# Keeping background work out of the step ahead of an accumulator copy, and computing the last output chunk in two halves

## The chip, the cores and the metric

The kernel is one program on one core of a Trainium2 chip. The metric is the device time of one execution in microseconds; of several executions the median is taken. The engines are named as in the profile: PE (matrix multiplications; PEld is its weight loads), DVE (the vector engine), ACT (the scalar engine), POOL (here the issuer of the stores to DRAM) and SP (the issuer of the loads and of the output stores). Each engine works through its own instructions strictly in order; an instruction that waits for a semaphore holds back all that stand behind it on that engine.

## What is computed

```python
# attention, B,H,S,Ns,D = 4,8,512,32,64, both ways, with softmax
xread = softmax(x @ state.T / 8) @ state      # x rows
sread = softmax(state @ x.T / 8) @ x          # state rows
x = concat(xread, sread)  ->  (2304, 512)
# first MLP, 512 -> 2048 -> 512
h = x @ w_in;  x = (h - tanh(h)) @ w_out
# second MLP, 512 -> 2048 -> 512
h = x @ w_in2; out = (h * tanh(softplus(h))) @ w_out2
```

The weights of the program arrive as 64-bit floats and are read as pairs of 32-bit words. The result is 32-bit.

## The kernel before, in words

Products are made to near 32-bit precision out of three products of a large part and a small remainder (`mm3p`, line 647): large x large, large x small, small x large. So nearly every tensor is split first: ACT copies the large part (names ending in `h`: `gh`, `wh`, `swh`, `yh`), and DVE subtracts it to get the rest (`gl`, `wl`, `swl`, `yl`).

The first MLP is a loop of 68 steps (lines 1217 to 1226), over `seq`: 16 tiles of 128 hidden columns for each of the batches 0, 1 and 2, then 4 tiles "s" for the state rows of all batches, then 16 tiles for batch 3. Batch 2 begins with step 32, "s" with step 48, batch 3 with step 52. A step does, in program order: `up` of its tile (6 matmuls into one of the two banks `h0`, `h1`; ACT takes the tanh, DVE subtracts it from the bank, which frees the bank, then ACT and DVE split it into `gh`, `gl`); the side work due at that step (the attention of the next batch; the products `swp`, whose two results lie in two side banks and are split into `swh`, `swl`; transposes `xtp`, which use the same two side banks in turn); `down` of a tile three steps back (`LA` is 3; near the end up to five), 12 matmuls into the four accumulator banks `a0` to `a3`; and `keep_pace` (line 1101), which runs some pieces of background work.

After the 16th `down` of a batch its four banks are copied out, two by ACT and two by DVE (line 713), and the first `down` of the next batch has to wait for these copies. That happens at steps 34 (batch 1), 50 (batch 2) and 54 (the state rows: one bank, `a3`, copied by ACT to `ys`, line 748).

A piece of background work converts or splits a part of the second MLP's weights and stores it to DRAM by POOL, from which it is loaded again later; or it prepares the second MLP's input of batches 0 and 1 (`pieces_y`). A conversion is two ACT operations on a loaded tile (`w<-st`, `r<-st`), one DVE operation and the load of a later tile; a split is one ACT and one DVE operation and two stores. There are 94 pieces. `keep_pace` runs them up to a goal that rises by 2.2 per step, at most `MOST` = 3 in a step (4 from step 58), and only while ten SBUF slots are free. Where a piece's new tile gets the slot of a tile that was stored, its first operation waits for the landing of that store.

After the first steps the order on an engine is not the program's: a scheduler places each instruction when its own count of time has its inputs ready. A piece can so stand on ACT or DVE ahead of an earlier step's operation.

The second MLP follows as 16 groups (`group`, line 940), PE-bound, with `down_2` (line 894) for the output chunks of 128 rows: 6 matmuls of 512 columns into one of three banks, then DVE adds the bank to the sum so far. In the last group the sum is stored. The very last chunk was computed like the others; only its addition and store were made in two halves of 256 columns (lines 921 to 925).

Of the kernel before, what the change touches and what calls it, by code (L numbers as in the profile page):

```python
# [17 lines left out]
LA = 3  # L18
# [8 lines left out]
MOST = 3  # L27
# [47 lines left out]
def attention_moe_kernel(  # L75
# [41 lines left out]
    def get(name, dtype=F32, newest=False):  # L117
        if halves and dtype == F32:
            return halves.popleft()
        i = free.pop() if newest else free.popleft()  # L120
        return Unit(slots.tile([128, 512], dtype, tag=f"k{i}", name=name), i)

    def put(*units):
        for u in units:
            if u.slot is None:
                halves.append(u)
            else:
                free.append(u.slot)
# [44 lines left out]
    last = [None]  # L173
# [74 lines left out]
    def run_piece():  # L248


        bg.popleft()()
        now[0] += 1
        send(now[0] - 1, now[0] - HOLD)

    def send(ready, gone):
        while stores and stores[0][0] < ready:
            _, u, d = stores.popleft()
            v = u.t.bitcast(F32)
            nc.gpsimd.dma_start(  # L259
                out=d, in_=v if len(d.shape) == 2 else v.rearrange("p (g e) -> p g e", g=2)  # L260
            )
            sent.append((now[0], u))
        while sent and sent[0][0] < gone:
            put(sent.popleft()[1])
# [382 lines left out]
    def mm3p(o, lh, ll, rh, rl, start, stop, **kw):  # L647
        TE.matmul(out=o, lhsT=lh, rhs=rh, start=start, stop=False, **kw)
        TE.matmul(out=o, lhsT=lh, rhs=rl, start=False, stop=False, **kw)
        TE.matmul(out=o, lhsT=ll, rhs=rh, start=False, stop=stop, **kw)  # L650
# [36 lines left out]
    def evac(dst, src, i):  # L687
        if i % 2:
            return V.tensor_copy(out=dst, in_=src)
        return AC.activation(out=dst, in_=src, func=ACTF.Copy)  # L690
# [139 lines left out]
    W2, O2, G2, OUT = {}, {}, {}, {}  # L830
# [63 lines left out]
    def down_2(g, b, r, gs, last):  # L894
        d_n[0] += 1
        ps = psum.tile([128, 512], F32, tag=DB[d_n[0] % len(DB)], name="acc")
        for f in range(2):
            if b == "s":
                gh, gl = (x.t[:, f * 128:(f + 1) * 128] for x in gs["s"])
            else:  # L900
                gh, gl = (x.t[:, r * 128:(r + 1) * 128] for x in gs[f, b % 2])
            wh, wl = O2[2 * g + f]
            mm3p(ps, gh, gl, wh.t, wl.t, f == 0, f == 1)
        if g == 0:
            OUT[b, r] = get("out")
            evac(OUT[b, r].t, ps, r)
            return
        o = OUT[b, r]
        if g < NT // 2 - 1:
            V.tensor_tensor(out=o.t, in0=ps, in1=o.t, op=ALU.add)  # L910
            return
        OUT.pop((b, r))
        if b == "s":
            V.tensor_tensor(out=o.t, in0=ps, in1=o.t, op=ALU.add)
            for bb in range(B):
                nc.sync.dma_start(
                    out=out[bb * T + S:(bb + 1) * T, :], in_=o.t[bb * NS:(bb + 1) * NS, :]
                )
        else:
            rows_out = out[b * T:b * T + S, :].rearrange("(p r) d -> p r d", r=4)[:, r, :]  # L920
            n = 2 if last else 1
            for j in range(n):
                c = slice(j * 512 // n, (j + 1) * 512 // n)
                V.tensor_tensor(out=o.t[:, c], in0=ps[:, c], in1=o.t[:, c], op=ALU.add)
                nc.sync.dma_start(out=rows_out[:, c], in_=o.t[:, c])
        put(o)
# [70 lines left out]
    def downs(u, g, with_s, last=False):  # L997
        gs = {k: G2.pop(k) for k in list(G2)}
        order = [(2 * u + 1, r) for r in range(4)]
        order += [("s", 0)] if with_s else []  # L1000
        order += [(2 * u, r) for r in range(4)]
        done = []

        def one(i):
            down_2(g, *order[i], gs, last and i == len(order) - 1)
            done.append(i)
            if len(done) == len(order):
                for x in gs.values():
                    put(*x)
                put(*O2.pop(2 * g), *O2.pop(2 * g + 1))  # L1010

        return [lambda i=i: one(i) for i in range(len(order))]
# [52 lines left out]
    start = {}  # L1065
# [35 lines left out]
    def keep_pace(i):  # L1101
        for (s0, n0), (s1, n1) in zip(pace, pace[1:]):
            if s0 <= i < s1:
                goal = n0 + (n1 - n0) * (i + 1 - s0) / (s1 - s0)
                ran = done[0]
                for _ in range(MOST + (i >= start[3] + 6)):
                    if done[0] < goal and bg and len(free) >= RESERVE:
                        run_piece()
                        done[0] += 1
                if ran == done[0]:  # L1110
                    now[0] += 3
                    send(now[0], now[0] - HOLD)
# [105 lines left out]
    for i, q in enumerate(seq):  # L1218
        marks.append([e.recent for e in engines])
        up(q)  # L1220
        for f in side.pop(i, []):
            f()
        while low <= i - LA - max(0, BACK - (len(seq) - 1 - i) // 2):
            down(seq[low])
            low += 1
        keep_pace(i)
# [65 lines left out]
```

## Time and profile before

| | us |
|---|---|
| median of 3 runs | 724.94 |
| lowest, highest | 724.18, 726.45 |
| the profiled execution itself | 724.73 |
| its span, first to last instruction | 723.0 |
| PE busy in the span | 709.4 |
| DVE busy, ACT busy | 465.6, 353.5 |

The granted clock of PE is 0.998 of full speed over the span, the upper of its two levels. The three runs lie 2.3 us apart. Nearly all instructions are recorded by one helper and carry its line, L62, so tiles tell them apart. Steps 30 to 68 of the first MLP lie from about 180 to 350 us, the second MLP behind them.

### The profile page before, as it was taken

The page shows a single profiled execution, that of the slowest core. Times are in us where ns is not written, and L with a number is a line of the kernel's source. Part 1 is how long each engine was busy: PE and PEld are TensorE (multiplying, and loading weights), DVE is VectorE, ACT ScalarE, POOL GpSimd, SP SyncE. Part 2 cuts the span into 40 slices and gives each one's busy share as a digit, 9 for nine tenths or more (in the row PEclk, how much of TensorE's full clock was granted, in tenths as well). Part 3 has the DMA queues.
Part 4 walks back from the last instruction along what each step waited for, and adds up shares of the span by engine and source line. Part 5 has one row for each costly group of instructions (what it writes and reads, how often), then busy time and mean ns, then how long its engine had stood idle before and what let it go on. Part 6 is the DMA issues. An engine that isn't in the chain of part 4 may idle for free.

```text
span 723.0 us, 10559 instructions
## 1 busy us (share of the span) xinstructions
PE 709.4 (98%) x3968; PEld 567.2 (78%) x3968; DVE 465.6 (64%) x793; ACT 353.5 (49%) x631; POOL 70.5 (10%) x110
## 2 busy tenths in 40 slices
PE   8899999999999999999999999999999999999997
PEld 6467877778777898777878888888788888888886
DVE  5899755575667748798557775556753365445654
ACT  6998455555675647676637332324433323222320
POOL 0000010012412214412004000000000000000000
PEclk9999999999999999999999999999999999999999
DMA  9984120023753439664958644454766354422003
GB/s 292 332 299 169 59 59 1 31 63 114 262 186 135 160 99 309 231 222 140 393 224 278 217 155 146 139 173 146 267 227 213 94 162 137 140 88 73 1 1 131
DMA packets 52643, 118.66 MB, mean 164 GB/s; under 512 B 7280, under 2 KB 11632, under 8 KB 52592
## 3 DMA queue, kind: packets, MB, share of 16 engines
q1 hardware_dynamic: 44272, 90.72, 38.4%
q0 software_dynamic: 8320, 27.27, 10.4%
q8 instruction: 31, 0.51, 0.3%
q14 instruction: 20, 0.16, 0.1%
HBM read 88.34 MB, written 29.62 MB: 163 GB/s over the span
## 4 chain that ended last, share of the span: by engine, by line
PE 68%; issue 13%; DVE 7%; ACT 6%; POOL 4%; DMA 0%; POOLq 0%; DVEq 0%; ACTq 0%
PE acc L62 35%; PE h L62 26%; POOL wi L259 3%; ACT w L62 2%; PE hs L62 2%; ACT r L62 1%; DVE wide L62 1%; DVE gl L62 1%; POOL wo L259 1%; PE xtp L62 1%; PE swp L62 1%; DVE yl L62 1%; PE srd L62 1%; DVE t L62 1%; DVE wl L62 1%
## 5 line engine op out<-in xcount | busy, mean ns | idle before, releaser
L62 PE MATMUL acc<-wo,gh 128*128 128x512 f32 x544 | 167.9, 390 | 0.0
L62 PE MATMUL h<-yh,ws 128*128 128x512 f32 x448 | 157.0, 392 | 0.5 <-DVE wide L62 0.5
L62 PEld LDWEIGHTS acc<-wo,gh 128*128 128x128 f32 x544 | 101.5, 188 | 21.1 <-ACT gh L62 0.5
L62 PE MATMUL acc<-wo,gl 128*128 128x512 f32 x272 | 106.0, 390 | 0.5 <-DVE gl L62 0.5
L62 DVE TENSOR_TENSOR wide<-acc,wide 128x512 f32<-128x512 f32 (+1 forms) x92 | 62.7, 684 | 62.5 <-PE acc L62 60.9
L62 PE MATMUL acc<-gh,wh 128*128 128x512 f32 x244 | 99.2, 407 | 0.7 <-ACT wide L62 0.4
L62 PEld LDWEIGHTS h<-yh,ws 128*128 128x128 f32 x448 | 84.1, 188 | 18.9 <-DVE wide L62 1.7
L62 PE MATMUL acc<-gh,wl 128*128 128x512 f32 x244 | 95.5, 391 | 0.0
L62 PE MATMUL acc<-gl,wh 128*128 128x512 f32 x244 | 95.4, 391 | 0.0
L62 DVE TENSOR_TENSOR wide<-h,wide 128x512 f32<-128x512 f32 x98 | 67.4, 688 | 31.8 <-ACT wide L62 18.8
L62 PE MATMUL h<-yl,ws 128*128 128x512 f32 x224 | 87.3, 390 | 0.0
L62 DVE TENSOR_TENSOR gl<-wide,gh 128x512 fp32r<-128x512 f32 x76 | 52.5, 690 | 37.7 <-ACT gh L62 36.8
L62 ACT ACTIVATE wide<-wide 128x512 f32<-128x512 f32 x47 | 29.7, 633 | 82.4 <-DVE wide L62 82.4
L62 ACT ACTIVATE wide<-h 128x512 f32<-128x512 f32 x45 | 26.7, 594 | 85.5 <-PE h L62 82.3
L62 PEld LDWEIGHTS acc<-gh,wh 128*128 128x128 f32 x244 | 45.8, 188 | 18.5 <-issue 6.4
L62 PEld LDWEIGHTS acc<-wo,gl 128*128 128x128 f32 x272 | 51.1, 188 | 11.7 <-DVE gl L62 1.0
L62 PE MATMUL h<-ath,swh 128*128 128x512 f32 x128 | 52.3, 408 | 2.2 <-DVE t L62 1.6
L62 PEld LDWEIGHTS acc<-gh,wl 128*128 128x128 f32 x244 | 45.8, 188 | 10.4 <-issue 0.4
L62 ACT ACTIVATE gh<-wide 128x512 fp32r<-128x512 f32 x76 | 48.0, 632 | 11.7 <-DVE wide L62 9.9
L62 PEld LDWEIGHTS acc<-gl,wh 128*128 128x128 f32 x244 | 45.9, 188 | 9.2 <-issue 0.8
L62 PE MATMUL h<-ath,swl 128*128 128x512 f32 x128 | 50.5, 394 | 0.1
L62 PE MATMUL h<-atl,swh 128*128 128x512 f32 x128 | 50.4, 394 | 0.0
(161 smaller groups left out, 1021.5 us busy)
## 6 DMA issues: line engine op xcount, KB each, us to landing
ws<-wi SPq DMA_DIRECT2D x128, 256.0 KB, 3.4
wo<-wo SPq DMA_DIRECT2D x64, 256.0 KB, 3.7
st<-in_moe_w_in_dram SPq DMA_DIRECT2D x27, 512.0 KB, 5.4
st<-in_moe_w_out_dram SPq DMA_DIRECT2D x22, 512.0 KB, 5.1
wi<-wh POOLq DMA_DIRECT2D x32, 256.0 KB, 4.0
wi<-wl POOLq DMA_DIRECT2D x32, 256.0 KB, 4.6
wide<-in_moe_w_out_dram SPq DMA_DIRECT2D x10, 512.0 KB, 5.1
wo<-wh POOLq DMA_DIRECT2D x16, 256.0 KB, 5.0
```

Source lines behind the costliest of these rows:

```text
L62: i = fn(*args, **kw)
L259: nc.gpsimd.dma_start(out=d, in_=v if len(d.shape) == 2 else v.rearrange("p (g e) -> p g e", g=2))
```

## The change

`keep_pace` runs no pieces in steps 33, 49 and 53, each the step before one with a copy of accumulators, and may run 4 pieces in a step from step 46 on (before: from 58). `down_2` computes the last chunk in two halves of 256 columns: 6 matmuls, addition and store for the first, then the same for the second, in the same bank.

```diff
--- before.py
+++ after.py
@@ -894,13 +894,20 @@
     def down_2(g, b, r, gs, last):
         d_n[0] += 1
         ps = psum.tile([128, 512], F32, tag=DB[d_n[0] % len(DB)], name="acc")
-        for f in range(2):
-            if b == "s":
-                gh, gl = (x.t[:, f * 128:(f + 1) * 128] for x in gs["s"])
-            else:
-                gh, gl = (x.t[:, r * 128:(r + 1) * 128] for x in gs[f, b % 2])
-            wh, wl = O2[2 * g + f]
-            mm3p(ps, gh, gl, wh.t, wl.t, f == 0, f == 1)
+        n = 2 if last else 1
+        parts = [slice(j * 512 // n, (j + 1) * 512 // n) for j in range(n)]
+
+        def sums(c):
+            for f in range(2):
+                if b == "s":
+                    gh, gl = (x.t[:, f * 128:(f + 1) * 128] for x in gs["s"])
+                else:
+                    gh, gl = (x.t[:, r * 128:(r + 1) * 128] for x in gs[f, b % 2])
+                wh, wl = O2[2 * g + f]
+                mm3p(ps[:, c], gh, gl, wh.t[:, c], wl.t[:, c], f == 0, f == 1)
+
+        if not last:
+            sums(parts[0])
         if g == 0:
             OUT[b, r] = get("out")
             evac(OUT[b, r].t, ps, r)
@@ -918,9 +925,9 @@
                 )
         else:
             rows_out = out[b * T:b * T + S, :].rearrange("(p r) d -> p r d", r=4)[:, r, :]
-            n = 2 if last else 1
-            for j in range(n):
-                c = slice(j * 512 // n, (j + 1) * 512 // n)
+            for c in parts:
+                if last:
+                    sums(c)
                 V.tensor_tensor(out=o.t[:, c], in0=ps[:, c], in1=o.t[:, c], op=ALU.add)
                 nc.sync.dma_start(out=rows_out[:, c], in_=o.t[:, c])
         put(o)
@@ -1103,7 +1110,8 @@
             if s0 <= i < s1:
                 goal = n0 + (n1 - n0) * (i + 1 - s0) / (s1 - s0)
                 ran = done[0]
-                for _ in range(MOST + (i >= start[3] + 6)):
+                ends = (start[x] + LA - 2 for x in (2, "s", 3))
+                for _ in range(0 if i in ends else MOST + (i >= start["s"] - 2)):
                     if done[0] < goal and bg and len(free) >= RESERVE:
                         run_piece()
                         done[0] += 1
```

The same pieces run in the same order, at other steps. As the programs are built, these are the pieces that had been run at the end of a step:

| step | 32 | 33 | 34 | 46 | 48 | 49 | 52 | 53 | 57 | 61 | 63 | 66 |
|---|---|---|---|---|---|---|---|---|---|---|---|---|
| before | 12 | 15 | 15 | 33 | 39 | 42 | 51 | 54 | 66 | 82 | 88 | 94 |
| now | 12 | 12 | 13 | 28 | 36 | 36 | 48 | 48 | 64 | 80 | 88 | 94 |

PE's own order is the same but for the last chunk. On ACT and DVE the order differs from step 33 to 68. Three places:

On ACT ahead of the copies of batch 1's accumulators (steps 33 and 34; `wide<-h` is a tanh, `DMASW` a landing of a store, `DMAHW` of a load). Before:

```order
L62 ACTIVATE wide<-st 128x512 [waits DMAHW6_49,Activation_49]
L62 ACTIVATE wide<-h 128x512 [waits PE_49]
L62 ACTIVATE gh<-wide 128x512 [waits DVE_49]
L62 ACTIVATE wide<-st 128x512 [waits DVE_49]
L62 ACTIVATE wh<-wide 128x512 [waits DMASW5_49,DVE_49]
L62 ACTIVATE wide<-h 128x512 [waits PE_49,Activation_49]
L62 ACTIVATE swh<-swp 128x512 [waits DMASW0_49,PE_49]
L62 ACTIVATE gh<-wide 128x512 [waits DVE_49]
L62 ACTIVATE swh<-swp 128x512 [waits PE_49]
L62 ACTIVATE w<-st 128x512 [waits DMAHW1_49,DMASW0_49]
L62 ACTIVATE wide<-acc_1307 128x512 [waits DVE_49,PE_49]
```

Now:

```order
L62 ACTIVATE wide<-h 128x512 [waits PE_49,Activation_49]
L62 ACTIVATE gh<-wide 128x512 [waits DVE_49]
L62 ACTIVATE w<-st 128x512 [waits DMAHW0_49,DMASW4_49,Activation_49]
L62 ACTIVATE r<-st 128x512 [waits DMASW5_49,DMASW1_49]
L62 ACTIVATE wide<-h 128x512 [waits PE_49]
L62 ACTIVATE swh<-swp 128x512 [waits PE_49]
L62 ACTIVATE wh<-w 128x512 [waits DMASW6_49,DVE_49]
L62 ACTIVATE gh<-wide 128x512 [waits DVE_49]
L62 ACTIVATE swh<-swp 128x512 [waits PE_49]
L62 ACTIVATE wide<-acc_1307 128x512 [waits PE_49,Activation_49]
```

The conversion that stood directly ahead of the copies (`w<-st`) is gone from there. Another conversion, of a later piece, stands ahead of step 34's tanh, and its two operations wait for stores; its split `wh<-w` stands between the two `swh`.

On ACT ahead of the copy of the state rows' accumulator (step 54). Before:

```order
L62 ACTIVATE t<-h 128x512 [waits PE_49]
L62 ACTIVATE wh<-s_3202 128x512 [waits PE_49]
L62 ACTIVATE swh<-swp 128x512 [waits PE_49]
L62 ACTIVATE gh<-t 128x512 [waits DVE_49]
L62 ACTIVATE swh<-swp 128x512 [waits DMASW6_49,PE_49]
L62 ACTIVATE yh<-wide 128x512 [waits DMASW4_49]
L62 ACTIVATE ys<-acc_3085 128x512 [waits PE_49]
```

Now:

```order
L62 ACTIVATE t<-h 128x512 [waits DMASW6_49,PE_49]
L62 ACTIVATE r<-st 128x512 [waits DMAHW5_49,PE_49]
L62 ACTIVATE swh<-swp 128x512 [waits PE_49]
L62 ACTIVATE gh<-t 128x512 [waits DMASW7_49,DVE_49]
L62 ACTIVATE swh<-swp 128x512 [waits PE_49,Activation_49]
L62 ACTIVATE w<-st 128x512
L62 ACTIVATE w<-st 128x512 [waits DMAHW7_49,DMASW2_49]
L62 ACTIVATE r<-st 128x512 [waits DMASW3_49]
L62 ACTIVATE wh<-w 128x512 [waits DVE_49]
L62 ACTIVATE ys<-acc_3064 128x512 [waits PE_49]
```

In place of one `yh<-wide`, which waits for a store, four operations of pieces of step 54 stand ahead of `ys`, which is earlier in the program.

On PE at the end: the last chunk. Before:

```order
L62 MATMUL acc<-wo,gh 128x512 [waits DVE_49]
L62 MATMUL acc<-wo,gh 128x512
L62 MATMUL acc<-wo,gl 128x512
L62 MATMUL acc<-wo,gh 128x512 x2
L62 MATMUL acc<-wo,gl 128x512
```

Now:

```order
L62 MATMUL acc<-wo,gh 128x256 [waits DVE_49]
L62 MATMUL acc<-wo,gh 128x256
L62 MATMUL acc<-wo,gl 128x256
L62 MATMUL acc<-wo,gh 128x256 x2
L62 MATMUL acc<-wo,gl 128x256
L62 MATMUL acc<-wo,gh 128x256 [waits DVE_49]
L62 MATMUL acc<-wo,gh 128x256
L62 MATMUL acc<-wo,gl 128x256
L62 MATMUL acc<-wo,gh 128x256 x2
L62 MATMUL acc<-wo,gl 128x256
```

The first matmul of the second half has a wait for DVE that the old chunk has only at its start: it waits for the addition of the first half, which reads the same bank.

## Rows read from the trace of the kernel before

**Rows 1.** The page, part 1: busy time, share, instructions
```profile
PE 709.4 (98%) x3968; PEld 567.2 (78%) x3968; DVE 465.6 (64%) x793; ACT 353.5 (49%) x631; POOL 70.5 (10%) x110
```

**Rows 2.** PE's waits, 150 to 420 us: total, times, longest
```profile
PE h L62 <- DVE wide L62: 0.6, 1, 0.6
...
PE acc L62 <- ACT wide L62: 0.4, 1, 0.4
...
PE acc L62 <- ACT ys L62: 0.2, 1, 0.2
```

**Rows 3.** Timeline of PE: start, us, what, [idle before <-releaser]
```profile
196.07 0.60 PE L62 MATMUL xtp<-ident,x 128*128 128x128 f32 x4
...
197.09 0.50 PE L62 MATMUL acc<-gh,wh 128*128 128x512 f32 x1 [0.42 <-ACT wide L62]
```

**Rows 4.** Timeline of ACT, 188 to 197 us
```profile
188.20 0.63 ACT L62 ACTIVATE gh<-wide 128x512 fp32r<-128x512 f32 x1 [0.76 <-DVE wide L62]
...
191.55 0.58 ACT L62 ACTIVATE wide<-h 128x512 f32<-128x512 f32 x1
...
195.86 0.69 ACT L62 ACTIVATE w<-st 128x512 f32<-128x512 f32 x1 [1.85 <-DMA wo<-wh]
...
196.45 0.58 ACT L62 ACTIVATE wide<-acc 128x512 f32<-128x512 f32 x1
```

**Rows 5.** Timeline of POOL: store issues
```profile
187.03 0.73 POOL L259 DMA_DIRECT2D wi<-wh  x1
...
187.76 0.72 POOL L259 DMA_DIRECT2D wi<-wl  x1
```

**Rows 6.** The page, part 6: DMA issues; last column us to landing
```profile
wi<-wh POOLq DMA_DIRECT2D x32, 256.0 KB, 4.0
...
wi<-wl POOLq DMA_DIRECT2D x32, 256.0 KB, 4.6
```

**Rows 7.** Timeline of PE, 225 to 227 us
```profile
226.02 0.33 PE L62 MATMUL sc<-ident,wide 128*128 128x128 f32 x1 [0.20 <-ACT scs L62]
...
226.53 0.55 PE L62 MATMUL sc<-ident,wide 128*128 128x128 f32 x3 [0.19 <-DVE wide L62]
```

**Rows 8.** Timeline of ACT, 220 to 225 us
```profile
224.24 0.66 ACT L62 ACTIVATE r<-st 128x512 uint32<-128x512 uint32 x1 [3.12 <-DMA wi<-wl]
```

**Rows 9.** Timeline of ACT, 300 to 304 us
```profile
300.56 0.60 ACT L62 ACTIVATE swh<-swp 128x512 fp32r<-128x512 f32 x1
...
302.54 0.63 ACT L62 ACTIVATE yh<-wide 128x512 fp32r<-128x512 f32 x1 [1.37 <-DMA wi<-wl]
...
303.07 0.58 ACT L62 ACTIVATE ys<-acc 128x512 f32<-128x512 f32 x1
```

**Rows 10.** Timeline of PE, 303 to 304 us
```profile
303.71 0.50 PE L62 MATMUL acc<-gh,wh 128*128 128x512 f32 x1 [0.23 <-ACT ys L62]
```

**Rows 11.** Busy time: stretch, length, PE, PEld, DVE, ACT, POOL (instructions), granted clock, DMA share, GB/s
```profile
304.00:342.00 38.00, 37.69 (x189) 28.95 (x188) 35.68 (x59) 28.38 (x52) 7.86 (x14) 1.00 0.56 184
```

**Rows 12.** Timeline of PE, 341 to 348 us
```profile
342.31 0.50 PE L62 MATMUL h<-ath,swh 128*128 128x512 f32 x1 [0.62 <-DVE wide L62]
...
347.89 0.39 PE L62 MATMUL h<-ath,swh 128*128 128x512 f32 x1
```

**Rows 13.** Timeline of DVE, 341 to 347 us
```profile
346.37 0.68 DVE L62 TENSOR_TENSOR wide<-h,wide 128x512 f32<-128x512 f32 x1
```

**Rows 14.** PE groups by line, shapes apart: busy us, mean ns
```profile
L62 PE MATMUL hs<-ws,yh 128*128 128x256 f32 x64 | 11.8, 282 | 0.0
```

**Rows 15.** Timeline of PE, DVE and SP's queue at the end
```profile
716.31 4.13 SPq L925 DMA_DIRECT2D out_dram<-wide  x5
...
717.62 0.62 PE L62 MATMUL acc<-wo,gh 128*128 128x512 f32 x2
...
718.76 0.39 PE L62 MATMUL acc<-wo,gl 128*128 128x512 f32 x1
...
719.18 0.76 DVE L62 TENSOR_TENSOR wide<-acc,wide 128x256 f32<-128x256 f32 x2 [0.67 <-PE acc L62]
```

## The prediction

> **What bounds the kernel now.** I read the page's busy times first: PE is busy for 709.4 of the 723.0 us of the span, 98% [rows 1]. No other engine is near that, so this is a kernel of PE work with a few holes, and an edit that leaves PE's work alone can only give or take holes, and time behind PE's last matmul. Next I read PE's waits for the stretch from 150 to 420 us, which holds all the steps that the change touches. They name three holes [rows 2]: one wait of 0.4 for an accumulator copy by ACT, one of 0.2 for the copy `ys`, one of 0.6 for the tanh subtraction on DVE. The timeline places the first at 197.09, idle 0.42 [rows 3], the first `down` of batch 2 (step 34); the second at 303.71, idle 0.23 [rows 10], step 54; the third at 342.31, idle 0.62 [rows 12]. Two short ones of 0.20 and 0.19 stand in the attention scores at 226.02 and 226.53 [rows 7]. No wait of that kind stands at step 50: of the three copies that the change protects, two cost PE anything.
>
> An idle time in a row is a little less than what the hole cost. In a full stream a matmul of 512 columns starts every (718.76 − 717.62) / 5 = 0.228 us, yet its record lasts 0.39 [rows 15]: 0.16 of each lies beside its successor, and a hole uncovers it. So the holes cost 0.42 + 0.16 = 0.58, twice 0.2 + 0.16 (together 0.71), 0.23 + 0.16 = 0.39 and 0.62 + 0.16 = 0.78: 2.46 us in all, 0.34% of the run. That is the most that can be won between steps 33 and 68.
>
> What ends the holes is read on ACT. Ahead of the copy at 196.45 stands a piece's `w<-st`, which waited 1.85 for a store's landing [rows 4]; ahead of `ys` at 303.07 a piece's `yh`, which waited 1.37 for one [rows 9]; ahead of the scores a piece's `r<-st`, which waited 3.12 [rows 8]. So pieces that wait for stores hold ACT, and what stands behind them. DVE is the other thing to watch: between 304 and 342 it is busy for 35.68 of 38.00 us with 59 operations [rows 11], so 2.3 us are spare, and the hole at 342.31 is where that runs out.
>
> **The change part by part.** *Step 33, the copy of batch 1.* The piece directly ahead of the copies goes, and with it 0.58 as far as that piece caused it. But the order now has another piece's `w`, `r` ahead of step 34's tanh, and both wait for stores. The stores that this slot needs were issued at 187.03 and 187.76 [rows 5]; such stores land 4.0 and 4.6 us after their issue [rows 6], at 191.0 and 192.4. The tanh that ran at 191.55 [rows 4] then starts behind `r`, at about 193.0. Behind it stand `swh`, `wh`, `gh`, `swh`: with 0.58 to 0.63 each the last ends at about 195.8, its subtraction on DVE at about 196.4. PE's transposes at 196.07 [rows 3] reuse that side bank, so they come some 0.3 late, which with 0.16 uncovered is 0.5 against the old 0.58: −0.1 us. Ends: −0.58, if the stores land at once; +0.6, if they land 1 us later than the mean.
>
> *The scores at 225.* With fewer pieces in flight after step 34 the one that waited 3.12 us need not stand there. I take −0.6 of 0.71. The nearest rows for the bad end are the same waits: if another piece's load or store of 1.4 to 3.1 us lands there, +0.8.
>
> *Step 49.* No hole at that copy, so nothing is won: 0. Three pieces fewer there are caught up at once by four per step, beside PE's stream; ends −0.2 and +0.4 (the price of a hole like those above).
>
> *Step 53, the copy `ys`.* The `yh` that waited 1.37 goes. Four operations of step 54's pieces come in its place, `w`, `w`, `r`, `wh`. From the end of the last `swh`, 300.56 + 0.60 = 301.16, four operations at ACT's pitch of 0.53 (302.54 to 303.07 [rows 9]) take until 303.28, where `ys` started at 303.07: +0.2. Ends: −0.39, if `ys` comes first after all; +1.4, if one of them waits for a store as `yh` did.
>
> *The catching up.* When step 53 ends, 48 pieces have run where 54 had. The six late ones, each with at least one DVE operation of 35.68 / 59 = 0.605 us [rows 11], bring 3.6 us to the stretch 304 to 345, where 2.3 are spare. The order shows them mostly behind the subtraction of the tanh that ended the hole at 342.31. There `up` of the next tiles has some room: the subtraction at 346.37 takes 0.68 [rows 13], ends at 347.05, and the `up` two steps on that takes its bank starts at 347.89 [rows 12]: 0.84 of slack. So D = 3.6 − 2.3 − 0.84 = +0.5. Ends: −0.8, if the subtraction ahead of 342.31 now comes before the backlog; +2.8, if the 2.3 spare can't be used, since DVE then waits for ACT and ACT for stores.
>
> *The last chunk.* In before, its six matmuls start at 717.62, the addition at 719.18, and both halves of the addition take until 719.94 [rows 15]. Now twelve of 256 columns: at half of 0.228 six take 0.68. The last of the first half starts at 717.62 + 5 × 0.114 = 718.19; a matmul of 256 columns has a record of 0.28 [rows 14], so the half is complete at 718.47 and its addition runs from 718.50 to about 718.90. The second half's first matmul has a wait for this addition. It starts at about 718.92, its last one at 719.49 and is complete at 719.77; with 0.1 for two hand-overs the second addition runs from about 719.9 to 720.3: +0.4 at the end. PE loses 0.7 to a wait in a place where nothing else is left to do. The store of the first half leaves 1.0 us sooner, but the program ends with the second: SP's queue is open until 716.31 + 4.13 = 720.44 [rows 15], right behind the last addition. If the halves could overlap, the last matmul would start at 718.87, the last addition would end at 719.6, and the edit would win 0.35. So the ends are −0.35 and +0.5; the order shows the wait, and I take +0.4.
>
> No row here has PE writing a bank while DVE reads it: the last addition starts after 0.67 idle, released by the last matmul [rows 15]. The Trainium skill, PSUM — Partial Sum Buffer, section "PSUM bank collisions raise a hardware error", says that two engines in one bank and the same 32 partitions at once raise an error, disjoint columns included. By that rule the wait can't be dropped while both halves share a bank, and the tail is +0.4; without it −0.35 would be open.
>
> **Sum.** The profiled execution took 724.73. −0.1 − 0.6 + 0 + 0.2 + 0.5 + 0.4 = +0.4, 725.1 us. The median of before, 724.94, lies 0.2 above the profiled run and the three runs are 2.3 apart, so I leave it there.
>
> **The rivals.** *Every wait goes.* All holes of 2.46 close and the halves overlap: 724.73 − 2.46 − 0.35 = 721.9. For it: each hole has a piece of the kind that the change moves. Against: the new order still has pieces with store waits ahead of steps 34 and 54, and the wait in the last chunk is there. I give 0.18, since pieces that arrive later might find their stores long landed.
>
> *Slower: the backlog on DVE.* One mechanism: the six late pieces come to the stretch that is 94% busy (35.68 of 38.00), the subtraction that frees the `up` bank stands behind them, and PE waits at 342 and again at the next `up`s. With 3.6 us of work, none of the spare time usable and 0.84 of slack, PE waits 2.8 more; with 0.4 at the tail and the other terms at nothing that is 724.73 + 2.8 + 0.4 = 727.9. For it: PE waits there already, and this is the one hole that DVE makes. Against: the late pieces stand largely behind that subtraction. It decides once the subtraction comes over 2.4 us later against PE than now. 0.22.
>
> *The change doesn't do what it says.* Pieces of other steps fill the place, since the order on an engine is not the program's: the same holes for other reasons, and only the last chunk counts: 724.73 + 0.4 = 725.1. For it: both places on ACT show just that. 0.15, beside my forecast's 0.45, in which holes close and open.
>
> **Numbers.** A measurement of this kernel can tell 0.3%, 2.2 us: faster is under 722.8, slower over 727.1. The forecast's own range, with the terms at half their way to the ends, is 723.5 to 726.8. Of the forecast and of the third rival all counts as the same (0.60), of the first rival all as faster (0.18), of the second all as slower (0.22). The range for 8 in 10 goes from 722.4, most of the way to the first rival, to 728.0, just past the second.
>
> **What would show it.** In the changed profile: the wait for an accumulator copy at 197 gone, and a wait of the transposes in its place (if neither is there, the first term is −0.58); no wait in the scores at 225; `ys` within 0.3 of where it was; DVE over 95% busy between 304 and 345 and PE's wait for the subtraction there moved by a few steps, not longer than 1.5; PE's last `down` split by a hole of 0.7 with one addition in it. I am wrong if PE waits over 2 us between 304 and 350, or if the holes between 190 and 350 are gone altogether.

## The result, and the profile after

The changed kernel takes 731.88 us against 724.57 of the kernel before, each the median of six runs: ratio 1.0094, interval 1.0079 to 1.0110. It is slower by 7.3 us where I forecast +0.4. Its profiled execution took 733.12, with a span of 731.4, so the trace shows some 1.2 us more than the median.

PE has 3.7 us more busy time and is 97% busy instead of 98% [rows 1]:

```profile
PE 713.1 (97%) x3974; PEld 569.7 (78%) x3974; DVE 466.0 (64%) x793; ACT 352.8 (48%) x631; POOL 70.5 (10%) x110
```

The same waits of PE as [rows 2], from 150 to 420 us. One of 3.5 for `swl` has come, and the subtraction makes two of 1.9 in all instead of one of 0.6; the waits for the copies `wide` and `ys` are gone:

```profile
PE h L62 <- DVE swl L62: 3.5, 1, 3.5
PE h L62 <- DVE wide L62: 1.9, 2, 1.3
PE xtp L62 <- DVE swl L62: 0.6, 1, 0.6
...
PE acc L62 <- ACT w L62: 0.4, 1, 0.4
```

PE's order is the same up to the last chunk, so the same matmul can be found in both traces, and the difference of its two times says what was lost by then. The next rows are PE's timeline after (start, duration, what, idle time and what ended it):

```profile
196.96 0.66 PE L62 MATMUL xtp<-ident,x 128*128 128x128 f32 x4 [0.60 <-DVE swl L62]
197.37 0.47 PE L62 MATMUL acc<-gh,wh 128*128 128x512 f32 x1
...
283.74 0.47 PE L62 MATMUL acc<-wh,gh 128*128 128x512 f32 x1 [0.40 <-ACT w L62]
...
303.49 0.39 PE L62 MATMUL acc<-gh,wh 128*128 128x512 f32 x1
...
325.86 0.80 PE L62 MATMUL h<-ath,swh 128*128 128x512 f32 x1 [3.46 <-DVE swl L62]
326.46 0.63 PE L62 MATMUL h<-atl,swh 128*128 128x512 f32 x1
...
328.56 0.63 PE L62 MATMUL h<-ath,swl 128*128 128x512 f32 x1
...
347.82 0.50 PE L62 MATMUL h<-ath,swh 128*128 128x512 f32 x1
...
352.75 0.50 PE L62 MATMUL h<-ath,swh 128*128 128x512 f32 x1 [0.55 <-DVE wide L62]
...
355.70 0.50 PE L62 MATMUL h<-ath,swh 128*128 128x512 f32 x1 [1.30 <-DVE wide L62]
```

197.37 answers to 197.09 [rows 3] and 303.49 to 303.71 [rows 10]; 347.82 and 355.70 answer to 342.31 and 347.89 [rows 12]. So the changed kernel was 0.28 behind after step 34, 0.22 ahead at step 54, 5.51 behind at 347.82 and 7.81 behind at 355.70. Nearly all is lost between 304 and 356, and most of it in one hole of 3.46 and right behind it: the rows 326.46 and 328.56, in a stream without waits, last longer than 0.39. The stretches show why (columns as in [rows 11]; the eighth number is the granted clock, the ninth the DMA share):

```profile
310.00:322.00 12.00, 12.00 (x65) 9.00 (x64) 6.12 (x11) 4.75 (x10) 4.47 (x9) 1.00 0.97 361
322.00:326.00 4.00, 0.54 (x3) 0.14 (x1) 3.32 (x6) 3.54 (x7) 0.00 (x0) 0.83 0.07 27
326.00:331.00 5.00, 4.97 (x11) 3.48 (x12) 5.00 (x9) 3.25 (x7) 0.00 (x0) 0.50 0.00 0
```

In the hole PE does next to nothing, and then it runs five microseconds at a granted clock of 0.50, the lower level. A matmul starts every 0.43 there instead of 0.228. From 322.01 to 331.5 PE loses 6.6 us, 3.6 in the hole and the rest at the lower clock.

What made the hole is read backwards. PE waits for `swl` on DVE, DVE for ACT. ACT's timeline:

```profile
313.75 0.62 ACT L62 ACTIVATE yh<-wide 128x512 fp32r<-128x512 f32 x1
321.27 0.63 ACT L62 ACTIVATE yh<-wide 128x512 fp32r<-128x512 f32 x1 [6.90 <-DMA wo<-wl]
321.81 0.61 ACT L62 ACTIVATE gh<-t 128x512 fp32r<-128x512 f32 x1
...
323.37 0.57 ACT L62 ACTIVATE t<-h 128x512 f32<-128x512 f32 x1
...
325.23 0.58 ACT L62 ACTIVATE swh<-swp 128x512 fp32r<-128x512 f32 x1
```

The second split `yh` is a piece of `pieces_y`. It stood 6.90 us for the landing of a store `wo<-wl`, and behind it stood the `gh`, the tanh and both `swh` of the next tiles. Which store that was, the chain of work that ended last tells (start, duration, what); the row of POOL that issued it stands first:

```profile
311.24 0.54 POOL L259 DMA_DIRECT2D wo<-wl  x1
```

```profile
311.24 10.01 DMA wo<-wl
321.24 0.02 issue
321.27 0.63 ACT yh L62
```

POOL issued it at 311.24, without a wait, and it took 10.01 us to land. In that stretch the DMA share is 0.97 (first row of the stretches), where before has 0.68 from 310 to 322. What fills the DMA engines there is not settled: POOL issues ten stores from 303 to 312, where before has seven, but f3 below has ten as well, and ACT waits for none of them.

PE's last waits, 0.55 and 1.30 near the end of the first MLP, are for the subtraction on DVE. DVE is not full there, nor in the stretch from 304 on, where in before it was busy for 94% up to 342 [rows 11] (columns as above):

```profile
304.00:345.00 41.00, 37.51 (x176) 28.17 (x175) 32.88 (x55) 26.41 (x49) 9.41 (x15) 0.92 0.51 176
345.00:356.00 11.00, 9.15 (x39) 6.75 (x38) 8.68 (x15) 6.16 (x12) 5.69 (x8) 1.00 0.88 301
```

The tail of PE and DVE, which answers to [rows 15]:

```profile
725.67 0.40 PE L62 MATMUL acc<-wo,gh 128*128 128x256 f32 x2
...
727.05 0.50 PE L62 MATMUL acc<-wo,gh 128*128 128x256 f32 x2 [0.52 <-DVE wide L62]
...
728.07 0.42 DVE L62 TENSOR_TENSOR wide<-acc,wide 128x256 f32<-128x256 f32 x1 [1.07 <-PE acc L62]
```

The second half's first matmul waits 0.52 for the first half's addition. From the chunk's first matmul to the end of the last addition it takes 725.67 to 728.49, 2.82, against 2.32 before (717.62 to 719.94): +0.50.

### The profile page after: what moved, and what is told of

The parts are those of the page before. It is cut to its first block, busy times and chain, and to the rows that moved or that the text cites. A ratio compares the mean times of both kernels' runs of the same rounds, so it can differ in the third digit from the quotient of the medians.

```text
span 731.4 us, 10569 instructions
## 1 busy us (share of the span) xinstructions
PE 713.1 (97%) x3974; PEld 569.7 (78%) x3974; DVE 466.0 (64%) x793; ACT 352.8 (48%) x631; POOL 70.5 (10%) x110
## 4 chain that ended last, share of the span: by engine, by line
PE 77%; DVE 8%; ACT 7%; issue 3%; DMA 3%; POOL 1%; ACTq 0%; POOLq 0%; DVEq 0%
PE acc L62 41%; PE h L62 28%; DVE wide L62 2%; DMA wo<-wl 2%; ACT w L62 2%; ACT r L62 2%; DVE gl L62 2%; PE hs L62 2%; PE swp L62 1%; PE xtp L62 1%; DVE yl L62 1%; PE srd L62 1%; PE sct L62 1%; DVE swl L62 1%; ACT gh L62 1%
## 5 line engine op out<-in xcount | busy, mean ns | idle before, releaser
L62 PE MATMUL acc<-wo,gh 128*128 128x512 f32 (+1 forms) x548 | 168.4, 389 | 0.5 <-DVE wide L62 0.5
L62 DVE TENSOR_TENSOR wide<-acc,wide 128x512 f32<-128x512 f32 (+1 forms) x99 | 67.7, 685 | 66.4 <-PE acc L62 64.9
L62 PE MATMUL acc<-wo,gl 128*128 128x512 f32 (+1 forms) x274 | 106.4, 388 | 0.5 <-DVE gl L62 0.5
L62 DVE TENSOR_TENSOR gl<-wide,gh 128x512 fp32r<-128x512 f32 x73 | 50.4, 690 | 36.0 <-ACT gh L62 35.9
L62 ACT ACTIVATE wide<-h 128x512 f32<-128x512 f32 x41 | 24.4, 594 | 78.3 <-PE h L62 77.8
L62 DVE TENSOR_TENSOR t<-h,t 128x512 f32<-128x512 f32 x52 | 35.7, 687 | 24.9 <-ACT t L62 24.9
```

What stands on the lines that cost most here:

```text
L62: i = fn(*args, **kw)
```

## The experiments

The kernel before ran again beside each experiment, and each ratio is against it on the same chip, with its 95% interval. The diffs are cut to the lines that matter.

**The two halves of the change, and the halves of the pacing.** The first keeps only `down_2` of the change, the second puts its second half into another bank:

```diff
+    if c.start:
+        ps = psum.tile([128, 512], F32, tag=DB[(d_n[0] + 1) % len(DB)], name="acc")
+    sums(c, ps)
```

> Only the last chunk in two halves; the pieces run as before. The trace of the changed kernel has the last chunk from 725.67 to the end of the last addition at 728.49, 2.82 us, against 2.32 before. Theory: the tail alone costs 0.5 us (0.0 to 0.9, within what can be measured here) and the 7 us come from the pieces. Rival: the new last chunk also changes the places of instructions elsewhere, then 2 us or more are seen.

725.48 against 724.77, 1.0009 [0.9995, 1.0023]. Its trace has the same hole of 0.52 and the same 2.82 from 718.66 to 721.48. So the tail can be 1.7 us at most (the interval's upper end), 0.5 by the trace, and the rest of the 7 us is the pieces'.

> As the kernel with the tail alone, but the second half goes into the next accumulator bank, so its matmuls need not wait for the first addition. Theory (the wait of 0.52 is for the shared bank): the hole in PE goes, the last addition ends 0.3 to 0.4 us sooner after the last chunk's first matmul than in the kernel before (2.32), -0.3 us. Rival (the halves must wait for each other in any case, or the first addition is late): the same hole as with one bank, +0.5.

1.0007 [0.9994, 1.0020]: not to be told from before by the times; the trace tells. PE and DVE at its end:

```profile
722.50 0.40 PE L62 MATMUL acc<-wo,gh 128*128 128x256 f32 x2
...
723.81 0.28 PE L62 MATMUL acc<-wo,gl 128*128 128x256 f32 x1
724.12 0.42 DVE L62 TENSOR_TENSOR wide<-acc,wide 128x256 f32<-128x256 f32 x1 [0.29 <-PE acc L62]
```

No hole; 722.50 to 724.54 is 2.04 where before has 2.32. The rival is out: the halves wait for each other only in a shared bank.

```diff
 e3  for _ in range(0 if i in ends else MOST + (i >= start[3] + 6)):
 e4  for _ in range(MOST + (i >= start["s"] - 2)):
```

> No pieces in steps 33, 49 and 53, but the rise to four a step at step 58 as before; old last chunk. By counting, 43 pieces have run at the end of step 53, where the kernel before has 54 and the changed one 48. Theory 1 (the rate of four pieces a step from step 46 on packs the stores, so that a slot is taken again before its store has landed): no wait of ACT over 3 us between 300 and 330, -1 to +2 us. Theory 2 (the six late pieces make the collision, whatever the rate): the wait is there or the backlog is worse, since more is late: +4 us or more.

> Four pieces a step from step 46 on, none left out; old last chunk. By counting, 61 pieces have run at the end of step 53, where the kernel before has 54. Theory 1 (rate): the pieces of y take slots whose stores were issued a step earlier, ACT waits some 4 to 7 us for a landing near the end of the weight pieces (then about 295 to 315) and PE 2 to 4 us: +3 to +8. Theory 2 (lateness by the skipped steps): nothing is late, PE's holes are as before: -1 to +1 us.

The empty steps alone take 733.64, 1.0119 [1.0102, 1.0135]; the rate alone takes 724.18, 0.9993 [0.9980, 1.0005]. Theory 1 fell: the higher rate is harmless, the empty steps are the loss. Without the higher rate the empty steps cost as much as with it (1.0119 and 1.0094, intervals that overlap). But theory 2 was not quite right either: the longest wait in e3 for a store is 2.55. ACT waits 4.17 for a load there, and PE loses at several places.

**Which empty step, and how late.**

```diff
 e5  HOLD = 8                        # was 6; the rest as changed
 e6  ends = (start[x] + LA - 2 for x in (2,))
 e7  ends = (start[x] + LA - 2 for x in ("s", 3))
 e8  ... MOST + 2 * (i >= start["s"] - 2)
```

> The changed kernel, but the slots of stored tiles are given back eight pieces later instead of six, so that a piece takes a slot whose store was issued longer ago. The pieces per step stay the same within one or two (28 at the end of step 46, 48 of step 53, as in the changed kernel). Theory A (the loss is the ACT wait of 6.90 for the landing of the store wo<-wl, behind which the tanh and the splits of two steps stand): that wait goes, with it PE's hole of 3.46 at 322 and the low clock after it; 731.9 falls to 725 to 728. Theory B (the six late pieces fill DVE and PE waits for it in any case): the same 730 to 733, with the hole at another subtraction.

730.73, 1.0085 [1.0061, 1.0109]. The hole at 322 is gone, as theory A has it, but step 34 now has one of 2.06 and PE stands 1.59 at 346. The time is the one of theory B. The edit moved the waits; ACT's for DMAs behind 270 went from 9.6 to 7.5 us in all.

> Only step 33 runs no pieces; four a step from step 46 on; old last chunk. By counting, 32 pieces have run at the end of step 47 (before 36, changed kernel 32), 56 of step 53 (before 54, changed kernel 48). Theory A (what counts is how many pieces are left for the steps from 53 on, when the input of the second MLP is prepared too): nothing late there, so -1 to +1.5 us against before. Theory C (the empty step 33 does it, by the order that it leaves behind): +4 us or more.

> Only steps 49 and 53 run no pieces; four a step from step 46 on; old last chunk. By counting, 41 pieces have run at the end of step 49 (before 42, changed kernel 36), 53 of step 53 (before 54, changed kernel 48). Theory A (pieces left at step 53): one piece late, -1 to +1.5 us. Theory D (the empty steps 49 and 53 themselves bunch the pieces of the next steps in front of the critical splits): +3 us or more.

> Steps 33, 49 and 53 run no pieces, five a step from step 46 on; old last chunk. By counting, 53 pieces have run at the end of step 53 (before 54, changed kernel 48). Theory A (pieces left at step 53): the loss of 7 us mostly goes, 724 to 727. Rival (more pieces in a step means more of them wait for stores and loads, and the hole of 3.46 comes back larger): 730 or more.

1.0119 [1.0088, 1.0151], 1.0087 [1.0053, 1.0120] and 1.0098 [1.0070, 1.0125]. Theory A in the form "pieces left at step 53" fell three times: e6 has two pieces more by then than the kernel before and is 9 us slower. Its first large hole stands at 283, and e7's first is there too. Step 33 alone (e6) costs as much as all three.

**Is it the one wait?**

```diff
+ send(now[0] - 1, now[0] - (HOLD if done[0] < 36 else 2 * HOLD))   # e9
+ (nc.sync if len(sent) % 2 else nc.gpsimd).dma_start(              # e10
```

> The changed kernel; from the 36th piece on the slots of stored tiles are given back twelve pieces later instead of six, and nothing is changed ahead of that (step 48). The pieces per step are those of the changed kernel. Theory A (the 6.0 us that PE loses from 322 to 332, hole and low clock, come from the one split of y that waits 6.90 on ACT for a store): that wait falls under 2 us, PE loses under 2 us there, and the kernel takes 725.5 to 728.5. Theory B (the late pieces hold DVE up, whatever ACT waits for): PE loses as much a few steps later, 730 to 733.

730.88, 1.0092 [1.0077, 1.0106]. The time is theory B's, but half of theory A held. The wait of 6.90 is gone, and with it the hole and the low clock: PE is busy in all of 322 to 332. But the waits of 0.56 and 1.29 for DVE at the end of the first MLP stay, as in the changed kernel, and a wait of 3.76 for a load now holds ACT at 290, `ys` comes late at 304, and PE stands 2.33 there. PE in e9:

```profile
305.07 0.52 PE L62 MATMUL acc<-gh,wh 128*128 128x512 f32 x1 [2.33 <-ACT ys L62]
```

ACT in e9, ahead of that:

```profile
290.78 0.66 ACT L62 ACTIVATE r<-st 128x512 uint32<-128x512 uint32 x1 [3.76 <-DMA st<-in_moe_w_in_dram]
...
298.68 0.63 ACT L62 ACTIVATE yh<-wide 128x512 fp32r<-128x512 f32 x1 [1.44 <-DMA wi<-wl]
...
304.43 0.59 ACT L62 ACTIVATE ys<-acc 128x512 f32<-128x512 f32 x1
```

The stretch behind the new hole, and the place of the old one, columns as above:

```profile
305.00:311.00 6.00, 5.93 (x21) 4.75 (x22) 5.81 (x12) 5.26 (x11) 4.37 (x7) 0.72 0.84 279
322.00:332.00 10.00, 10.00 (x46) 8.29 (x45) 10.00 (x18) 6.75 (x14) 1.08 (x2) 1.00 0.50 197
```

The hole follows the wait: where ACT stands long for a DMA just ahead of a split or copy, PE stands, and here too the clock is below full behind the hole (0.72).

> The changed kernel; every second store of a piece is issued by SP instead of POOL. In the changed kernel the store that ACT waits for was computed at 314.5, but issued at 317.41, since POOL issues each store only when the eighth one before it has landed; it landed at 321.2. Theory P (POOL's row of stores is what makes the wait long): ACT's wait of 6.90 is shorter by 2 to 3 us and PE's hole of 3.46 falls under 1.5, 726 to 729. Theory Q (the DMA engines are full there, busy share 0.97 to 1.0, so another queue changes nothing), or SP's loads come late behind waiting stores: 730 to 735.

733.49, 1.0129 [1.0116, 1.0142]. Theory P fell: with half of the stores on SP, ACT's wait is 6.15 instead of 6.90, PE's hole there is 2.45, and one of 2.23 has come at step 34. The theory rested on a wrong reading of mine: the store issued late, at 317.41, is not the one that ACT waited for. In e10 the awaited store is issued by SP, and it too is long on its way:

```profile
313.54 9.82 DMA wo<-wl
```

So the length of the wait is the landing, not POOL's row of stores.

> Only step 53 runs no pieces; four a step from step 46 on; old last chunk. Theory A (a piece with an open load or store must not stand on ACT ahead of a tight operation; one empty step moves few pieces): between the kernel with no empty step (-0.5 us) and the one with steps 49 and 53 empty (+6.9): 0 to +3. Theory C (any empty step costs the whole, by the order it leaves): +5 or more. If the empty step does what it is for: -0.5 to -1.

730.13, 1.0083 [1.0060, 1.0106], over runs from 727.5 to 734.3. Theory C: one empty step costs nearly the whole. It has the same pieces up to step 52 as e4 (0.9993), and yet its hole stands at 285, ahead of step 53. ACT there:

```profile
277.64 0.69 ACT L62 ACTIVATE w<-st 128x512 f32<-128x512 f32 x1 [1.58 <-DMA st<-in_moe_w_in_dram]
278.23 0.69 ACT L62 ACTIVATE r<-st 128x512 uint32<-128x512 uint32 x1
281.45 0.66 ACT L62 ACTIVATE r<-st 128x512 uint32<-128x512 uint32 x1 [2.53 <-DMA wi<-wh]
282.02 0.58 ACT L62 ACTIVATE t<-h 128x512 f32<-128x512 f32 x1
...
284.84 0.60 ACT L62 ACTIVATE y<-acc 128x512 f32<-128x512 f32 x1
```

In e4 no `r<-st` stands between this `w`, `r` and the tanh. Here one does, of a later piece, which waits 2.53 for a store; the copies of step 50 come late, and PE stands 2.29. So emptying step 53 changed the order three steps earlier: pieces are pulled forward.

An empty step does one more thing, which no run takes apart. The last lines of `keep_pace` move its count by three when no piece ran, and so issue stores and give back slots as if three had run. e5 and e9, which keep the slots longer, did not win the time back, so this is not the whole of it.

> Four pieces a step from step 46 on with no empty step, and the last chunk in two halves in two banks: the two parts that did not lose by themselves, put together. Both are small: ratio 0.9993 [0.998, 1.0005] for the first, and by the trace -0.27 us for the second (2.05 against 2.32 from the last chunk's first matmul to the end of the last addition). So -0.3 to -1.2 us, probably not to be told from the kernel before. Rival (the two interfere): over +0.5 us.

724.49, 0.9998 [0.9987, 1.0010]: no gain that can be told.

**What if nothing can be pulled ahead of the copies?** In these kernels pieces and all later work may stand on ACT and DVE only behind the step's own last operation:

```diff
+        if i in (34, 50, 54):              # f1; f2, f6: range(32, 68)
+            AC.floor = AC.recent           # f3 to f5: (32, 33, 34, 48, 49, 50, 52, 53, 54)
+            V.floor = V.recent
         keep_pace(i)
```

> The changed kernel; in steps 34, 50 and 54 the pieces (and all that is later in the program) may stand on ACT and DVE only behind the step's own last operation there, so that no later piece is pulled ahead of the copies. Theory H (the empty step does not protect the copy, because the order is made by a scheduler that pulls pieces of the next steps into the gap, and those wait for loads and stores): ACT's waits ahead of the three copies go, PE's holes at 196, 283 and 303 are 0 to 0.3. What remains is the wait for the store at 321 if the pieces still come in a bunch: 726 to 731 by that. Rival (the pieces' order ahead of the copies is of no account): the same 731 to 733.

> The same rule in each step from 32 to 67: no piece stands ahead of a tanh or split of its own step or of an earlier one. Theory H: most waits of ACT for a load or a store now stand where a step's own work is done, and PE's holes between 270 and 355 fall from 11 us to under 4: 723 to 728. Rival (without the pull forward the pieces stand just ahead of the next step's tanh, where they wait as long, and what the scheduler filled in is lost): 731 or more.

730.67, 1.0066 [1.0043, 1.0088], and 732.18, 1.0092 [1.0073, 1.0111]. Theory H is half right. In both, PE has no hole at the copies any more: at step 54 f1 is 1.63 ahead of the kernel before (302.08 for 303.71), f2 2.48 (0.56 of it from the first 100 us). Then it is lost again. f1, PE at step 54 and behind it:

```profile
302.08 0.39 PE L62 MATMUL acc<-gh,wh 128*128 128x512 f32 x1
...
330.80 0.50 PE L62 MATMUL h<-ath,swh 128*128 128x512 f32 x1 [4.30 <-DVE wide L62]
```

f2, where ACT waits for a DMA only once between 150 and 370, 1.63 us:

```profile
356.33 0.80 PE L62 MATMUL h<-yh,ws 128*128 128x512 f32 x1 [5.07 <-DVE wide L62]
```

There PE stands 5.07 for DVE at the very end of the first MLP, with the last conversions and splits ahead of the subtraction. From 342 to 356 DVE is busy for 11.84 of 14.00 us and ACT for 10.85: a backlog of both, with no DMA in it. The time of f2 is the rival's.

> The kernel before, with no step emptied; in steps 32 to 34, 48 to 50 and 52 to 54 pieces may stand on ACT and DVE only behind the step's own work. Theory H: the holes of 0.58 at 197 and 0.39 at 303 shrink and nothing new comes: -0.3 to -1.2 us. Rival (any change of order costs, since the order before was one that happened to have few waits): +3 or more.

722.83 against 725.57: 0.9963 [0.9948, 0.9978], faster than both kernels. PE's waits in it, as [rows 2]:

```profile
PE acc L62 <- DVE gl L62: 0.5, 1, 0.5
PE sc L62 <- ACT scs L62: 0.4, 1, 0.4
PE swp L62 <- ACT xt L62: 0.3, 1, 0.3
PE sc L62 <- DVE wide L62: 0.2, 1, 0.2
```

The copies and the subtraction are gone from the list, and ACT's waits for DMAs behind 270 are down to 0.2 us. So the copies can be protected, without an empty step. Its trace shows only a part of the gain: 1.3 us, from 0.35 behind the kernel before at 100 us to 0.98 ahead at 360.

> Four pieces a step from step 46, last chunk in two banks, no step emptied, and the rule of the run before in the same nine steps. Theory H: -0.5 to -2 us against before. Rival (any change of order costs): +3 or more.

729.08, 1.0050 [1.0030, 1.0069]: the rival. The same rule with four pieces a step has a `yh` that waits 3.34 for a store, and PE stands 4.25, with the granted clock at 0.56 from 316 to 323. The rule gives nothing by itself, then; the order must come out without such a wait.

> The kernel before with no empty step, pieces kept behind the step's own work on ACT and DVE in steps 32 to 34, 48 to 50 and 52 to 54 (which gave 0.9963 [0.9948, 0.9978]), and the last chunk in two halves in two banks (-0.27 us by its trace). If the two add: -2.5 to -3.3 us, ratio 0.9955 to 0.9966. Rival (the gain is that of one order that happened to be good): over 0.998.

> The kernel before with pieces kept behind the step's own work in each step from 32 to 67, no step emptied. In the changed kernel the same rule closed every hole up to 303 (PE 2.48 us ahead of the kernel before there) and lost 9 us behind it, from 342 on. Theory L (the loss behind is the six late pieces): here nothing is late, and the loss at the end of the first MLP is under 2 us: 721 to 725. Rival (the rule itself makes the pieces late, whatever the steps before): PE waits 3 us or more between 342 and 357 here too, 727 or more.

f5: 722.77, 0.9976 [0.9962, 0.9990]; faster again, but by less than the 0.9955 to 0.9966 that I expected if the two gains add, and just short of the rival's 0.998, so that f3's order was in part a lucky one is not ruled out. f6: 725.59, 1.0017 [1.0001, 1.0033], with PE waits of 2.8 at the end of the first MLP, between the two forecasts. f2 and f6 differ in the empty steps (with the rate and the tail), 1.0092 and 1.0017: without them the rule costs little.

**All runs together.** What ACT waited for loads and stores behind 270 us, summed over its timeline to 370, and the ratio:

| kernel | ACT waits for DMA, us | ratio |
|---|---|---|
| f5, f6, f3 | 0.0, 0.0, 0.2 | 0.9976, 1.0017, 0.9963 |
| e1, e12, e2, before, e4 | 2.7, 3.1, 3.1, 3.2, 3.6 | 1.0009, 0.9998, 1.0007, 1, 0.9993 |
| e7, e5, e9, e11 | 6.3, 7.5, 7.9, 8.0 | 1.0087, 1.0085, 1.0092, 1.0083 |
| f1, changed, e10, e3 | 9.6, 9.6, 10.0, 11.1 | 1.0066, 1.0094, 1.0129, 1.0119 |
| e8, e6 | 13.3, 14.0 | 1.0098, 1.0119 |
| f4, f2 | 3.3 (one wait), 1.6 | 1.0050, 1.0092 |

Above the last row the ratio rises with the sum, loosely: 9.6 stands at 1.0066 (f1) and 6.3 at 1.0087 (e7). Each sum is of one execution, while the ratio is of all; e7's was the fastest of its six (726.87, median 730.86). f4 has one wait, but with the hole of 4.25 and the low clock behind it; f2 has the backlog. So this is a relation that goes with the explanation, and no proof of it.

## Why the prediction was wrong

The time, 731.88, lies beyond my range (722.4 to 728.0) and on the side that I gave 0.22. By the terms, measured at the same matmuls:

- **Step 33**, −0.1: measured +0.14 (0.14 behind at 150 us already, 0.28 behind it). The mechanism was right: the wait for the copy gone, one of 0.60 of the transposes in its place.
- **Scores**, −0.6: measured −0.84: the waits of [rows 7] are gone, and the accumulator matmul behind them, at 226.84 before, stands at 226.28 (from +0.28 to −0.56). Right.
- **Step 49**, 0: a hole of 0.40, which the profile puts down to an ACT `w`, has come (283.74), where before had none; with what it uncovers 0.6, beyond my upper end of 0.4. The empty step ahead of a copy did not protect it.
- **`ys`**, +0.2: measured −0.40 (from 0.18 behind at 300 us to 0.22 ahead), its lower end. The four operations stood ahead of it as forecast, but early enough: `ys` started at 302.49, and PE's wait is gone.
- **The catching up**, +0.5, ends −0.8 and +2.8: measured −0.22 to +7.81, 8.0 us. This is the step that failed. I priced six late pieces as DVE time, 3.6 less 2.3 spare less 0.84 of slack. That counted what DVE computes, not what ACT waits for: DVE was busy for 32.88 of 41.00 us from 304 to 345, 80%, where my sign was over 95%. The late pieces came with the splits of `y` right behind the last stores, and one of these waited 6.90 for a landing; DVE stood 6.14 behind it and PE 3.46. No such wait is in my term; the longest of a `yh` in before is 1.37. And I priced no hole with the clock behind it: a hole of 3.46 cost 6.6. My own sign of being wrong, a wait of PE over 2 us between 304 and 350, is there.
- **The last chunk**, +0.4: measured +0.50. In one bank PE stood 0.52 (after and e1), in two it did not (e2). The Trainium skill, PSUM — Partial Sum Buffer, section "PSUM bank collisions raise a hardware error", has two engines in one bank and the same 32 partitions at once as an error; by that rule the wait could not be left out, only the bank changed. No run here shows the error itself.

Of the rivals the slower one had the right place, 304 to 356, and the right sign, but the waits for DVE's subtraction were the smaller part: from 5.51 to 7.81 between the two `up`s, 2.3 of the 7.8, with DVE busy for 8.68 of 11.00 us. The decisive part, a store's landing ahead of the tanh and splits on ACT, stood in my text only in the upper ends of this term (+2.8) and of `ys` (+1.4).

What stays open: why an empty step costs so much even where the count of pieces has caught up (e6). Shown is that the empty steps lose the time, and neither the rate (e4) nor the tail (e1); that emptying step 53 changes the order three steps ahead of itself (e11); and that in the changed kernel the hole at 322 goes with ACT's wait (e5, e9), though the time does not, since other waits come. That such waits are the whole loss in every kernel is argued, not shown; f2 loses as much with a single one of 1.63. What made the scheduler choose these orders was not tried.

## What to carry to other kernels

Work that is left out of a step is not gone: count where it lands, with its loads, stores and waits, not only with its compute time. An empty step ahead of a copy need not protect it where a scheduler fills the gap from later steps. Emptying the steps lost 0.94%; forbidding that order gave 0.37% and 0.24% (f3, f5), but lost 0.50% with four pieces a step (f4), so the trace after it has to be read as well. To the price of an operation that is moved on an in-order engine belongs the longest wait that it can bring to all that stands behind it, and a hole in PE's stream can have a second price in the clock.

## What the runs showed of the hardware

- The clock can take nearly as much as the hole: behind 3.46 us of idle PE ran over five us at a granted clock of 0.50. The length of the hole alone does not tell whether it comes. It fell behind holes of 2.06 (e5), 2.29 (e11) and 2.33 (e9), and not behind one of 1.30 (355.70 in the changed kernel, 1.00 from 350 to 400); but it stayed at 1.00 behind 2.49 (e7) and behind 3.12 and 2.64 in e6. The first of e6, and the six us behind it (the eighth number is the clock):

```profile
287.00 0.47 PE L62 MATMUL acc<-wh,gh 128*128 128x512 f32 x1 [3.12 <-ACT wh L62]
```

```profile
287.00:293.00 6.00, 6.00 (x26) 4.96 (x27) 4.81 (x10) 3.92 (x7) 2.99 (x5) 1.00 0.92 298
```

- The landing of a store depends on what else is moving: from 295 to 325 the stores `wo<-wl` took 8.1 us in the middle in the changed kernel and 6.2 in the kernel before. The one that ACT waited for took 10.01, with the DMA share at 0.97.
